# A three-stage transformer stack on one core: when the third and fourth batch's attention starts, and which engine makes the low weight parts

## The chip, the core and the metric

One core of one Trainium2 chip. The time is that of one execution in device microseconds; the kernel before was run three times. One of these runs was also profiled, and every number below that is not one of the three times is of that execution. TensorE is called PE in the rows, VectorE DVE, ScalarE ACT, GpSimd POOL and SyncE SP; SP only issues DMAs here.

## The reference

```python
# 1. attention over 32 memory slots: 4 batches, 8 heads, 576 tokens, head width 64
a = softmax(phi, axis=2)                       # over the tokens' 32 slots
k_m, v_m = a.T @ k, a.T @ v                    # per batch and head: 32 x 64
attn = softmax(q @ k_m.T / 8) @ v_m            # 2304 rows of 512
# 2. a dense layer pair, 512 -> 2048 -> 512, with ELU
h = x @ w_in
x = where(h > 0, h, exp(min(h, 0)) - 1) @ w_out
# 3. eight experts, 512 -> 1024 -> 512, two per token
logits = x @ w_gate + log1p(exp(x @ w_noise)) * noise
# the best two experts of each token, softmax of their logits as weights
out[mask] += weight * (relu(x[mask] @ w1[e]) @ w2[e])
```

## The kernel before

Everything is one loop over 160 iterations. Iterations 0 to 63 are the dense pair: 16 per block of tokens (blocks of 4, 5, 4 and 5 tiles of 128 tokens, one block per batch, `u["blk"]`), and each makes 128 of the 2048 hidden features. Iterations 64 to 159 are the experts. An iteration `i` of the dense pair holds, on PE, `layer1` (L992: 12 matmuls in two halves, each half into one of two PSUM banks called `ph`), and then `layer2` (L1042 to L1044) of iteration `i - 2`: for each tile of the block three matmuls of 512 columns into that tile's accumulator bank `acc`. The products are split: each operand is a high part (`bh`, `gh`, `ah`, `th`) and a low part (`bl`, `gl`, `al`, `tl`), and three of the four cross products are summed. ACT takes two exponentials out of `ph` (L997, L998) and DVE finishes the ELU (L1006, then L1007, which reads `ph`); only when L1007 has read a half is its bank free for the next iteration's `layer1`. The high part of the weight chunk that `layer2` will need two iterations later is made by ACT (L571), the low part by `prep_lo` (L577).

The attention of batch 1, 2 and 3 is no stage of its own. `attention(b)` is a Python generator; `tick` is called at three places of an iteration (before `layer1`, `""`; within it, `"mid"`; and at the end, `"late"`) and lets the generator go one step, if the kind of step that it asked for (`"pe"`, `"light"`, `"next"`, `"late"`, ...) fits the place. A step puts a few instructions into the engines' queues there. Two queues of generators matter: `heads` (the attention, and the last gating) goes first, `tails` (the gating of blocks 0 and 1) after it. A batch's attention pools phi, k and v (L175 transposes, L193), takes scores (L314 into a side bank, L322 to L324 on DVE), normalizes them (L338 to L341), turns them back (L345) and makes high and low parts (`tl`, L350).

The side work on PE needs PSUM banks besides the accumulators. While a block of 5 tiles is in `layer2` there is one only, `px` (`single()`); with 4 tiles there are two, `px` and `acc4`. The folding of the attention's values into the first layer's weights (`fold`, L491, every fourth iteration) uses them too: ACT and DVE take `fh` and `fl` out of the banks (L137, L138).

The gating (`gating(blk, ...)`, L652 to L815) of a finished block runs beside the next block: logits (L642), top two experts, positions by a matmul with a triangle of ones (L768 to L772, one step, one side bank), then on POOL the slots (L786 to L806) and one small indirect DMA per 128 entries (L815), paced by `beat` (L624): at most two per iteration. The engines run their queues in order, so an instruction that waits holds all behind it on its engine.

Of the kernel before, what the change touches and what calls it, by code (L numbers as in the profile page):

```python
# [9 lines left out]
F32 = mybir.dt.float32  # L10
# [5 lines left out]
OP = mybir.AluOpType  # L16
# [4 lines left out]
P = 128  # L21
NB, NH, S, HD, NM = 4, 8, 576, 64, 32
# [4 lines left out]
H = S // 2  # L27
# [15 lines left out]
def moe_stack_kernel(ctx, tc, phi, kv, kvt, q, wmlp, wgn, noise, wmoe, out):  # L43
# [27 lines left out]
    def single():  # L71
        return len(banks["tags"]) == 1
# [42 lines left out]
    def att_loads(b):  # L115
        return ([lambda: load_phi(b)] + [lambda w=w, c=c: load_kv(b, w, c) for w in range(2) for c in range(2)]
                + [lambda h=h: load_q(b, h) for h in range(2)])
# [21 lines left out]

    def attention(b):  # L140
        first = b == 0
        for _ in range(0 if first else 1 if b == 1 else 2):
            yield "gap"
        ph = att["phi", b]
        nmx = sm.tile([P, 2], F32, tag="nmx", name="nmx")
# [110 lines left out]
        sbs = {}  # L256
# [75 lines left out]
        def grow_t(h, g):  # L332
            act.activation(sbs[h, g], sbs[h, g], AF.Exp, scale=0.125)

        def normalize_t(h, g):
            sb = sbs[h, g]
            su = sm.tile([P, 16], F32, tag="ssu", name="ssu", bufs=2)[:, :H // 32]
            dve.tensor_reduce(out=su, in_=sb, axis=AX, op=OP.add)  # L338
            dve.tensor_scalar(su, su, 1e-9, None, op0=OP.add)
            dve.reciprocal(su, su)  # L340
            (dve if b == 3 else pool).tensor_tensor(sb, sb, su[:, :, None].to_broadcast([P, H // 32, NM]), op=OP.mult)  # L341

        def turn_t(h, g):
            back = sbs[h, g, "back"] = ap_.tile([P, 1024], F32, tag="cvm", name="back", bufs=2)[:, :H]
# [2 lines left out]

        def lower_t(h, g):
            hi, lo = (t[:, g, h * H:(h + 1) * H] for t in xt)
            dve.tensor_tensor(lo, sbs[h, g, "back"], hi.bitcast(F32), op=OP.subtract)  # L350

        if first:
            scores(0)
            grow(0)
            scores(1)
            grow(1)
            load_to(3)
            keep([("a", 0), ("a", 1)])
            load_phi(1)
            pooled([1])  # L360
            normalize(0)
            scores(2)
            across([1])
            conv1_hi(pieces(0))
            normalize(1)
            warm(2)
            fold_half(0)
            grow(2)
            normalize(2)
            warm(3)  # L370
            turn(0)
            conv1_lo(pieces(0))
            warm(4)
            turn(1)
            turn(2)
            conv2(pieces(0))
            conv1_hi(pieces(1))
            conv1_lo(pieces(1))
        elif b >= 2:
            yield "gap"  # L380
            for h in range(2):
                if single():
                    if h:
                        grow_t(0, 0)
                    scores_t(h, [0])
                    yield
                    if h:
                        grow_t(0, 1)
                    scores_t(h, [1])
                    yield "next" if h else "pe"  # L390
                else:
                    for g in range(2):
                        scores_t(h, [g])
                        yield "late"
                        grow_t(h, g)
                        if (h, g) != (1, 1):
                            yield "mid"
            if (1, 0) in sbs and single():
                grow_t(1, 0)
                grow_t(1, 1)  # L400
            q0, q1, q2, q3 = [(h, g) for h in range(2) for g in range(2)]
            for steps in ([(normalize_t, q0)], [(normalize_t, q1)], [(turn_t, q0), (turn_t, q1)],
                          [(normalize_t, q2)], [(lower_t, q0), (lower_t, q1)], [(normalize_t, q3)],
                          [(turn_t, q2), (turn_t, q3)], [(lower_t, q2), (lower_t, q3)]):
                yield "light"
                for step, q in steps:
                    step(*q)
        else:
            scores(0)
            yield "late"  # L410
            grow(0)
            yield
            scores(1)
            yield "late"
            grow(1)
            normalize(0)
            yield
            scores(2)
            yield "late"
            grow(2)  # L420
            normalize(1)
            yield
            turn(0)
            yield "late"
            normalize(2)
            yield
            turn(1)
            yield
            turn(2)
# [143 lines left out]
    def prep_lo(parts):  # L573

        for h, c in parts:
            hi, lo = ready[h, c]
            dve.tensor_tensor(lo, raws.pop((h, c)), hi.bitcast(F32), op=OP.subtract)  # L577

# [7 lines left out]
    def tick(slot="", taken=False):  # L588


        place[0] = slot
        kinds = {"": {"pe", "light", "next"}, "mid": {"pe", "mid"}, "late": {"late", "light"}}[slot]
        kinds = kinds - ({"pe", "mid"} if taken else set())
        went = False
        for queue in (heads or tails, tails, sides):
            if queue is sides and slot == "mid" and not taken and not (went and single()):
                kinds = {"mid"}
            while queue:
                gen = queue[0]
                want = wants.get(id(gen)) or {"fetch": "next", "tiles": "late"}.get(gen.__name__, "pe")  # L600
                if want == "gap":
                    if slot != "late":
                        wants[id(gen)] = None
                    break
                if want not in kinds or want == "next" and stepped.get(id(gen)) == i:
                    break
                stepped[id(gen)] = i
                went = True
                try:
                    wants[id(gen)] = next(gen)  # L610
                    if moe.get("pair") or slot == "late":
                        kinds -= {"pe"} & {want}
                    else:
                        kinds -= {want} - {"next"} if slot == "" else kinds
                    break
                except StopIteration:
                    wants.pop(id(queue.pop(0)), None)
# [41 lines left out]
    def gating(blk, rows):  # L659
# [102 lines left out]
        wts = rec.bitcast(F32)  # L762
        if eng is pool:
            pool.tensor_scalar(den, e2, 1.0, 1e-9, op0=OP.add, op1=OP.add)
        yield "next" if blk < 2 else "pe"
        last = blk == len(BLOCKS) - 1
        bk = side_bank()
        pe.matmul(bk[:, :nt * NE + NE].rearrange("p (t e) -> p t e", e=NE), ones,  # L768
# [359 lines left out]
    for i in range(len(flat)):  # L1128
# [3 lines left out]
        if i < len(flat):  # L1132
# [22 lines left out]
                            route(m, flat.index((m, 0)))  # L1155
            if k == late + 4 and f == 2:
                tails.append(overflow_table())
            if k in (1, 2) and f == 0:
                paced = att_loads(k + 1) + paced
            if k < 3 and f == 0:  # L1160
                n = units[k + 1]
                n["need"] = attention(k + 1)
                heads.append(n["need"])
            if k and u["kind"] == "mlp" and f == 0:
                u["x"] = att["x", k]
            j = (i + 2) // 4
# [182 lines left out]
```

## Time and profile before

| what | value |
|---|---|
| three runs: median, lowest, highest | 866.58, 866.22, 867.23 us |
| the profiled execution's time | 866.58 us |
| its span, first to last instruction | 864.8 us |
| PE busy, share of the span | 840.4 us, 97% |
| DVE | 567.5 us, 66% |
| ACT | 438.3 us, 51% |
| POOL | 205.5 us, 24% |
| PE's granted clock over the span | 0.998 of full speed |

The profiled execution is the median run itself; 1.8 us of its time lie outside the span. Busy shares are averages over stages: the dense pair ends at about 400 us and the experts fill the rest. A matmul's busy time ends later than the moment at which the next one can start, so gaps on PE are read from start to start as well.

### The profile page before, as it was taken

Reading aid. Unit: us, or ns where it says so; the run is one execution under the profiler, and the core shown is the slowest. Engines: PE = TensorE matmul, PEld = TensorE weight load, DVE = VectorE, ACT = ScalarE, POOL = GpSimd, SP = SyncE. Lnnn points to the kernel's source line nnn. Section 1 sums busy time; section 2 is a strip of 40 time slices with the busy share of each in tenths; the row PEclk is TensorE's granted clock in tenths of the full one; section 3 lists DMA queues with packets and bytes.
Section 4 is the critical chain, followed back from the end, with each engine's and each line's share of the span. In section 5 each row is a group of like instructions: output and inputs, shape, how many; then the busy total and the mean of one; then the engine's idle time right before and its main releaser. Section 6 shows DMA issues by size and latency. Waiting matters only on the chain. (4 is left out here: it accounts for less than half of the span.)

```text
span 864.8 us, 15414 instructions
## 1 busy us (share of the span) xinstructions
PE 840.4 (97%) x5688; PEld 695.7 (80%) x5691; DVE 567.5 (66%) x1200; ACT 438.3 (51%) x1007; POOL 205.5 (24%) x319
## 2 busy tenths in 40 slices
PE   8999999999999899999999999999999999999995
PEld 5566668777877678888888998898899999899994
DVE  4878888589778897687787664654757354453321
ACT  4867666555655565555656544444534243332311
POOL 0100100002306535031545430341431050110303
PEclk9999999999999999999999999999999999999999
DMA  9996678964852436364898987879995674542404
GB/s 340 362 388 227 223 270 270 325 242 155 298 165 99 98 137 157 99 207 128 245 230 231 283 239 271 226 206 282 257 271 140 197 178 144 160 108 98 60 1 60
DMA packets 100575, 174.65 MB, mean 202 GB/s; under 512 B 14610, under 2 KB 52370, under 8 KB 99474
## 3 DMA queue, kind: packets, MB, share of 16 engines
q1 hardware_dynamic: 90514, 152.93, 55.3%
q0 software_dynamic: 9984, 20.72, 11.7%
q8 instruction: 45, 0.74, 0.4%
q14 instruction: 32, 0.26, 0.1%
HBM read 132.01 MB, written 41.61 MB: 201 GB/s over the span
## 5 line engine op out<-in xcount | busy, mean ns | idle before, releaser
L1042 PE MATMUL acc<-bh,gl 128*128 128x512 f32 (+1 forms) x552 | 219.6, 398 | 0.6 <-DVE rows L1063 0.5
L1043 PE MATMUL acc<-bl,gh 128*128 128x512 f32 (+1 forms) x552 | 216.6, 392 | 0.0
L1044 PE MATMUL acc<-bh,gh 128*128 128x512 f32 (+1 forms) x552 | 216.0, 391 | 0.0
L1021 DVE SCALAR_TENSOR_TENSOR gl<-ph,gh 128x312 fp32r<-128x312 f32 (+2 forms) x128 | 61.5, 481 | 191.8 <-ACT gh L1020 191.8
L571 ACT ACTIVATE bh<-raw 128x512 fp32r<-128x512 f32 x144 | 89.9, 624 | 72.5 <-PE acc L1044 72.4
L1042 PEld LDWEIGHTS acc<-bh,gl 128*128 128x128 f32 (+1 forms) x552 | 102.8, 186 | 26.2 <-issue 6.5
L1044 PEld LDWEIGHTS acc<-bh,gh 128*128 128x128 f32 (+1 forms) x552 | 102.8, 186 | 23.7
L1020 ACT ACTIVATE gh<-ph 128x312 fp32r<-128x312 f32 (+2 forms) x128 | 54.8, 428 | 126.1 <-PE ph L992 125.9
L1043 PEld LDWEIGHTS acc<-bl,gh 128*128 128x128 f32 (+1 forms) x552 | 102.8, 186 | 17.1
L1065 POOL DMA_INDIRECT out<-rows,ids x40 | 64.9, 1622 | 187.8 <-DVE rows L1063 168.0
L577 DVE TENSOR_TENSOR bl<-raw,bh 128x512 fp32r<-128x512 f32 x144 | 99.0, 687 | 5.6 <-ACT bh L571 5.6
L992 PE MATMUL ph<-xl,ah 128*128 128x312 f32 (+2 forms) x512 | 95.2, 308 | 0.0
L992 PE MATMUL ph<-xh,al 128*128 128x312 f32 (+2 forms) x512 | 94.2, 306 | 0.0
L992 PE MATMUL ph<-xh,ah 128*128 128x312 f32 (+2 forms) x512 | 93.5, 305 | 0.0
L992 PEld LDWEIGHTS ph<-xl,ah 128*128 128x128 f32 x512 | 83.5, 189 | 8.9
L992 PEld LDWEIGHTS ph<-xh,al 128*128 128x128 f32 x512 | 79.4, 188 | 0.0
L992 PEld LDWEIGHTS ph<-xh,ah 128*128 128x128 f32 x512 | 78.9, 188 | 0.0
L992 PE MATMUL ph<-tl,fh 128*128 128x288 f32 x256 | 60.5, 317 | 6.3 <-DVE elu L1007 4.7
L577 DVE TENSOR_TENSOR al<-raw,ah 128x512 fp32r<-128x512 f32 x96 | 65.4, 681 | 0.0
L1006 DVE SCALAR_TENSOR_TENSOR elu<-elu 128x288 f32<-128x288 f32 x128 | 58.5, 457 | 9.4 <-ACT elu L998 9.4
L936 POOL DMA_INDIRECT xg<-x2d,ids x35 | 37.3, 1066 | 112.7 <-DMA ids<-lst 70.4
L1013 ACT ACTIVATE gh<-elu 128x576 fp32r<-128x576 f32 (+1 forms) x50 | 33.0, 660 | 58.4 <-DVE elu L1007 58.4
(263 smaller groups left out, 1243.4 us busy)
## 6 DMA issues: line engine op xcount, KB each, us to landing
raw<-in_wmoe SPq DMA_DIRECT2D x48, 1024.0 KB, 6.7
raw<-in_wmlp SPq DMA_DIRECT2D x32, 512.0 KB, 7.2
raw<-wxa SPq DMA_DIRECT2D x12, 1024.0 KB, 6.9
raw<-wxb SPq DMA_DIRECT2D x12, 1024.0 KB, 7.6
xs<-xg SPq DMA_DIRECT2D x35, 256.0 KB, 8.6
xq<-xs SPq DMA_DIRECT2D x140, 64.0 KB, 4.4
kv<-in_kv SPq DMA_DIRECT2D x8, 1024.0 KB, 10.2
out<-zrow SPq DMA_DIRECT2D x13, 512.0 KB, 9.7
```

What stands on the lines that cost most here:

```text
L571: act.activation(ready[h, c][0], raws[h, c], AF.Copy)
L577: dve.tensor_tensor(lo, raws.pop((h, c)), hi.bitcast(F32), op=OP.subtract)
L936: pool.indirect_dma_start(out=xg, out_offset=None, in_=x2d[:rows], in_offset=bass.IndirectOffsetOnAxis(ap=n["ids"][:, t, 0:1], axis=0))
L992: pe.matmul(ph, w, x, start=k == 0, stop=k == len(terms) - 1)
L1006: dve.scalar_tensor_tensor(m, t[:, 0, o], 1.0, m, op0=OP.add, op1=OP.mult)
L1013: act.activation(gh[:, o], m, AF.Copy)
L1020: act.activation(gh[:, o], ph, AF.Relu)
L1021: dve.scalar_tensor_tensor(gl[:, o], ph, 0.0, gh[:, o].bitcast(F32), op0=OP.max, op1=OP.subtract)
L1042: pe.matmul(acc, gl[:, o], wh, start=f == 0, stop=False)
L1043: pe.matmul(acc, gh[:, o], wl, start=False, stop=False)
L1044: pe.matmul(acc, gh[:, o], wh, start=False, stop=f == u["nf"] - 1)
L1065: d = pool.indirect_dma_start(out=out, out_offset=bass.IndirectOffsetOnAxis(ap=ids[:m, t, 0:1], axis=0), in_=r, in_offset=None, compute_op ...
```

## The change

Four things, all in iterations 9 to 63. The attention of batch 2 is handed to `heads` in iteration 13 in place of 16 and that of batch 3 in iteration 26 in place of 32 (its two "gap" steps fall away as well, so its first step comes in iteration 13 and about iteration 25 to 26), and the loads of phi, k, v and q for them are queued in iterations 9 and 23. The scores and exponentials of these two batches are written so that a step fits both one and two side banks. In iterations 16 to 63 the low part of layer 2's weight chunk (L577) is made by GpSimd instead of VectorE, and so are the attention's low parts (L350) of batches 2 and 3 and batch 3's normalization (L341). The gating's position step of blocks 0 and 1 gets a kind of its own, `"bank"`, which is not taken in a `tick` whose iteration has just folded.

```diff
--- before.py
+++ after.py
@@ -139,7 +139,7 @@
 
     def attention(b):
         first = b == 0
-        for _ in range(0 if first else 1 if b == 1 else 2):
+        if b == 1:
             yield "gap"
         ph = att["phi", b]
         nmx = sm.tile([P, 2], F32, tag="nmx", name="nmx")
@@ -338,7 +338,7 @@
             dve.tensor_reduce(out=su, in_=sb, axis=AX, op=OP.add)
             dve.tensor_scalar(su, su, 1e-9, None, op0=OP.add)
             dve.reciprocal(su, su)
-            (dve if b == 3 else pool).tensor_tensor(sb, sb, su[:, :, None].to_broadcast([P, H // 32, NM]), op=OP.mult)
+            pool.tensor_tensor(sb, sb, su[:, :, None].to_broadcast([P, H // 32, NM]), op=OP.mult)
 
         def turn_t(h, g):
             back = sbs[h, g, "back"] = ap_.tile([P, 1024], F32, tag="cvm", name="back", bufs=2)[:, :H]
@@ -347,7 +347,7 @@
 
         def lower_t(h, g):
             hi, lo = (t[:, g, h * H:(h + 1) * H] for t in xt)
-            dve.tensor_tensor(lo, sbs[h, g, "back"], hi.bitcast(F32), op=OP.subtract)
+            pool.tensor_tensor(lo, sbs[h, g, "back"], hi.bitcast(F32), op=OP.subtract)
 
         if first:
             scores(0)
@@ -378,26 +378,26 @@
             conv1_lo(pieces(1))
         elif b >= 2:
             yield "gap"
+            raw_ = []
             for h in range(2):
                 if single():
-                    if h:
-                        grow_t(0, 0)
-                    scores_t(h, [0])
-                    yield
-                    if h:
-                        grow_t(0, 1)
-                    scores_t(h, [1])
-                    yield "next" if h else "pe"
-                else:
                     for g in range(2):
+                        if len(raw_) > 1:
+                            grow_t(*raw_.pop(0))
                         scores_t(h, [g])
-                        yield "late"
-                        grow_t(h, g)
-                        if (h, g) != (1, 1):
-                            yield "mid"
-            if (1, 0) in sbs and single():
-                grow_t(1, 0)
-                grow_t(1, 1)
+                        raw_.append((h, g))
+                        yield "next" if h and g else "pe"
+                    continue
+                for g in range(2):
+                    scores_t(h, [g])
+                    yield "late"
+                    for a in raw_ + [(h, g)]:
+                        grow_t(*a)
+                    raw_.clear()
+                    if (h, g) != (1, 1):
+                        yield "mid"
+            for a in raw_:
+                grow_t(*a)
             q0, q1, q2, q3 = [(h, g) for h in range(2) for g in range(2)]
             for steps in ([(normalize_t, q0)], [(normalize_t, q1)], [(turn_t, q0), (turn_t, q1)],
                           [(normalize_t, q2)], [(lower_t, q0), (lower_t, q1)], [(normalize_t, q3)],
@@ -574,7 +574,7 @@
 
         for h, c in parts:
             hi, lo = ready[h, c]
-            dve.tensor_tensor(lo, raws.pop((h, c)), hi.bitcast(F32), op=OP.subtract)
+            (pool if 15 < c < 64 else dve).tensor_tensor(lo, raws.pop((h, c)), hi.bitcast(F32), op=OP.subtract)
 
 
 
@@ -589,20 +589,20 @@
 
 
         place[0] = slot
-        kinds = {"": {"pe", "light", "next"}, "mid": {"pe", "mid"}, "late": {"late", "light"}}[slot]
-        kinds = kinds - ({"pe", "mid"} if taken else set())
+        kinds = {"": {"pe", "light", "next", "bank"}, "mid": {"pe", "mid"}, "late": {"late", "light"}}[slot]
+        kinds = kinds - ({"pe", "mid", "bank"} if taken else set())
         went = False
         for queue in (heads or tails, tails, sides):
             if queue is sides and slot == "mid" and not taken and not (went and single()):
                 kinds = {"mid"}
             while queue:
                 gen = queue[0]
-                want = wants.get(id(gen)) or {"fetch": "next", "tiles": "late"}.get(gen.__name__, "pe")
+                want = wants.get(id(gen)) or {"fetch": "next", "tiles": "late", "attention": "light" if id(gen) not in wants else "pe"}.get(gen.__name__, "pe")
                 if want == "gap":
                     if slot != "late":
                         wants[id(gen)] = None
                     break
-                if want not in kinds or want == "next" and stepped.get(id(gen)) == i:
+                if want not in kinds or want in ("next", "bank") and stepped.get(id(gen)) == i:
                     break
                 stepped[id(gen)] = i
                 went = True
@@ -762,7 +762,7 @@
         wts = rec.bitcast(F32)
         if eng is pool:
             pool.tensor_scalar(den, e2, 1.0, 1e-9, op0=OP.add, op1=OP.add)
-        yield "next" if blk < 2 else "pe"
+        yield "bank" if blk < 2 else "pe"
         last = blk == len(BLOCKS) - 1
         bk = side_bank()
         pe.matmul(bk[:, :nt * NE + NE].rearrange("p (t e) -> p t e", e=NE), ones,
@@ -1155,12 +1155,14 @@
                             route(m, flat.index((m, 0)))
             if k == late + 4 and f == 2:
                 tails.append(overflow_table())
-            if k in (1, 2) and f == 0:
-                paced = att_loads(k + 1) + paced
-            if k < 3 and f == 0:
-                n = units[k + 1]
-                n["need"] = attention(k + 1)
+            if i in (9, 23):
+                paced = att_loads(2 + i // 16) + paced
+            if i in (0, 13, 26):
+                n = units[1 + i // 13]
+                n["need"] = attention(1 + i // 13)
                 heads.append(n["need"])
+                if i == 0:
+                    wants[id(n["need"])] = None
             if k and u["kind"] == "mlp" and f == 0:
                 u["x"] = att["x", k]
             j = (i + 2) // 4
```

Where the instructions stand. The first place is PE's queue around the fold of iteration 18 (`ph` and `px` are PSUM banks, `raw` a weight chunk, `kmF` the pooled keys of batch 2, `acc` an accumulator). Before:

```order
L491 MATMUL ph<-raw,vT 32x512
L491 MATMUL px<-raw,vT 32x512
L1042 MATMUL acc_1537<-bh,gl 128x512
L1043 MATMUL acc_1537<-bl,gh 128x512
L1044 MATMUL acc_1537<-bh,gh 128x512
L992 MATMUL ph<-tl,fh 128x288 x2
```

and now:

```order
L491 MATMUL ph<-raw,vT 32x512
L491 MATMUL px<-raw,vT 32x512
L1042 MATMUL acc_1617<-bh,gl 128x512
L1043 MATMUL acc_1617<-bl,gh 128x512
L1044 MATMUL acc_1617<-bh,gh 128x512
L314 MATMUL px<-q,kmF 32x288 x4
L992 MATMUL ph<-tl,fh 128x288 x2
```

The scores of batch 2 now ask for `px` one tile after the fold has filled it. In the same way the position step of block 0, which stood behind a fold of iteration 39, stands in iteration 33 right behind scores of batch 3, and in the same bank:

```order
L314 MATMUL px<-q,kmF 32x288 x4
L768 LDWEIGHTS ones
L768 MATMUL px<-run,ones 128x40
L770 LDWEIGHTS tri
L770 MATMUL px<-g_oh,tri 128x32
L992 MATMUL ph<-tl,fh 128x288 x2
```

The second place is DVE's queue from the elementwise work of iteration 42 to that of 43. Before (the queue of PE has a fold in between, whose two L138 stand here):

```order
L1007 SCALAR_TENSOR_TENSOR elu<-ph,elu 128x288
L322 STREAM_TRANSPOSE sbt<-px 128x288
L323 TENSOR_REDUCE smx<-sbt 128x9
L324 TENSOR_TENSOR sbt<-sbt,smx 128x288
L138 TENSOR_TENSOR fl<-acc_3472,fh 128x512
L138 TENSOR_TENSOR fl<-px,fh 128x512
L338 TENSOR_REDUCE ssu<-sbt 128x9
L339 TENSOR_SCALAR ssu<-ssu 128x9
L340 RECIPROCAL ssu<-ssu 128x9
L341 TENSOR_TENSOR sbt<-sbt,ssu 128x288
L1025 TENSOR_TENSOR gl<-elu,gh 128x512
L577 TENSOR_TENSOR bl<-raw,bh 128x512
```

and now:

```order
L1007 SCALAR_TENSOR_TENSOR elu<-ph,elu 128x288
L712 RECIPROCAL g_r<-g_r 128x40
L138 TENSOR_TENSOR fl<-acc_3535,fh 128x512
L138 TENSOR_TENSOR fl<-px,fh 128x512
L1025 TENSOR_TENSOR gl<-elu,gh 128x512
L1006 SCALAR_TENSOR_TENSOR elu<-elu 128x288
```

The attention of batch 3 and the low part have left this stretch. The third place is POOL's queue after the slots of block 0. Before, the slots were followed by the entries alone, with nothing between them:

```order
L806 CAST g_slot_2571<-g_ss1_3206 128x4
L624 COPY tiny_101<-beat_3214 1x1
L815 DMA lst_89<-g_rec_2572,g_slot_2571 19328x2
L624 COPY tiny_101<-beat_3246 1x1
L815 DMA lst_89<-g_rec_2572,g_slot_2571 19328x2
```

and now (from the entry beside iteration 34 on):

```order
L577 TENSOR_TENSOR bl_2864<-raw_2405,bh_2863 128x512
L624 COPY tiny_101<-beat_2898 1x1
L815 DMA lst_89<-g_rec_2255,g_slot_2254 19328x2
L624 COPY tiny_101<-beat_2962 1x1
L815 DMA lst_89<-g_rec_2255,g_slot_2254 19328x2
L577 TENSOR_TENSOR bl_2948<-raw_2405,bh_2947 128x512
L341 TENSOR_TENSOR sbt_2708<-sbt_2708,ssu_2984 128x288
L624 COPY tiny_101<-beat_2989 1x1
L815 DMA lst_89<-g_rec_2255,g_slot_2254 19328x2
L341 TENSOR_TENSOR sbt_2708<-sbt_2708,ssu_3005 128x288
```

The low parts of iterations 34 and 35 and the first two normalizations of batch 3 now stand between the entries of block 0. DVE's transposes of what these two leave (L345) stand right behind the elementwise work of iteration 36, and the pair of the other two normalizations behind that of iteration 38.

## Rows read from the trace of the kernel before

**Rows 1.** The waits of PE: total us, times, longest us.

```profile
PE ph L992 <- DVE elu L1007: 4.7, 4, 1.7
...
PE acc L768 <- DVE fl L138: 1.5, 1, 1.5
...
PE ph L992 <- DVE fl L138: 0.5, 1, 0.5
```

**Rows 2.** Busy us (count) of PE, PEld, DVE, ACT, POOL in 40 us; clock; DMA.

```profile
280.00:320.00 40.00, 35.33 (x214) 27.93 (x213) 35.57 (x90) 22.28 (x65) 17.15 (x43) 1.00 0.39 106
```

**Rows 3.** PE in time: start us, us, line; a logits group, then an undisturbed iteration.

```profile
262.52 0.45 PE L642 MATMUL acc<-wgs,x2T 128*32 128x16 f32 x32
...
316.34 0.51 PE L992 MATMUL ph<-tl,fh 128*128 128x288 f32 x2
...
320.52 0.39 PE L1044 MATMUL acc<-bh,gh 128*128 128x512 f32 x1
320.75 0.42 PE L992 MATMUL ph<-tl,fh 128*128 128x288 f32 x2
```

**Rows 4.** DVE and PE in time, from the fold of iteration 43 to iteration 44.

```profile
284.63 0.68 DVE L138 TENSOR_TENSOR fl<-px,fh 128x512 fp32r<-128x512 f32 x1
...
288.87 0.50 PE L992 MATMUL ph<-tl,fh 128*128 128x288 f32 x2 [1.25 <-DVE elu L1007]
```

**Rows 5.** PE and DVE in time, the fold of iteration 15.

```profile
117.78 0.61 PE L491 MATMUL px<-raw,vT 64*32 64x512 f32 x1
...
120.19 0.68 DVE L138 TENSOR_TENSOR fl<-px,fh 128x512 fp32r<-128x512 f32 x1
```

**Rows 6.** PE in time, the fold of iteration 18 and iteration 19.

```profile
137.00 0.61 PE L491 MATMUL px<-raw,vT 64*32 64x512 f32 x1
...
138.81 0.43 PE L992 MATMUL ph<-tl,fh 128*128 128x288 f32 x2
```

**Rows 7.** PE and DVE in time, scores of batch 2.

```profile
171.80 0.69 PE L314 MATMUL px<-q,kmF 64*32 64x288 f32 x8
...
172.42 0.50 PE L1042 MATMUL acc<-bh,gl 128*128 128x512 f32 x1
172.56 0.48 DVE L322 STREAM_TRANSPOSE sbt<-px 128x288 f32<-128x288 f32 x1 [1.49 <-PE px L314]
```

**Rows 8.** Groups by line: count, busy us, mean ns, idle before.

```profile
L577 DVE TENSOR_TENSOR bl<-raw,bh 128x512 fp32r<-128x512 f32 x144 | 99.0, 687 | 5.6 <-ACT bh L571 5.6
L1006 DVE SCALAR_TENSOR_TENSOR elu<-elu 128x288 f32<-128x288 f32 x128 | 58.5, 457 | 9.4 <-ACT elu L998 9.4
L294 POOL TENSOR_TENSOR sb<-sb,ssu 128x512 f32<-128x512 f32 x4 | 4.2, 1049 | 88.7 <-ACT elu L998 63.3 <-DVE ssu L293 25.4
L341 POOL TENSOR_TENSOR sbt<-sbt,ssu 128x288 f32<-128x288 f32 x4 | 3.6, 911 | 102.4 <-ACT gh L1016 92.1 <-DVE ssu L340 9.6 <-PE ph L992 0.8
```

**Rows 9.** POOL and DVE in time, a normalization of batch 1.

```profile
95.53 1.05 POOL L294 TENSOR_TENSOR sb<-sb,ssu 128x512 f32<-128x512 f32 x1 [5.78 <-DVE ssu L293]
95.81 1.07 DVE L1006 SCALAR_TENSOR_TENSOR elu<-elu 128x288 f32<-128x288 f32 x1
```

**Rows 10.** POOL in time: noisy logits of block 0; its slots; its first entries.

```profile
224.27 0.31 POOL L693 TENSOR_SCALAR g_u<-g_u 128x32 f32<-128x32 f32 x1
...
232.94 0.41 POOL L729 TENSOR_TENSOR g_noisy<-g_noisy,lg 128x32 f32<-128x32 f32 x1
...
266.47 0.21 POOL L786 TENSOR_TENSOR g_rec<-g_rec,g_e 128x4 f32<-128x4 f32 x1 [4.31 <-DVE g_rec L785]
...
270.79 0.18 POOL L624 COPY tiny<-beat 1x1 f32<-1x1 f32 x1
...
275.97 0.17 POOL L624 COPY tiny<-beat 1x1 f32<-1x1 f32 x1
```

**Rows 11.** DVE in time, from a pair of L345 to the end of that iteration's work.

```profile
199.77 0.83 DVE L345 STREAM_TRANSPOSE back<-sbt 128x288 f32<-128x288 f32 x2
...
203.13 0.68 DVE L577 TENSOR_TENSOR bl<-raw,bh 128x512 fp32r<-128x512 f32 x1
```

## The prediction

> **What bounds the kernel now.** I read the page's busy shares first: PE is busy 840.4 of 864.8 us at a granted clock of 0.998 (the table), so the amount of matrix work is the bound, and the change adds and removes none: it moves instructions in PE's queue and takes elementwise work from one engine to another. What it can win is PE's idle time. So the next view is PE's own waits [rows 1]. The largest is `layer1` waiting for L1007: 4.7 us in four waits. It is a wait for a `ph` bank that DVE has not read yet, so DVE is late. Then 1.5 us in which the position step of block 0 (L768) waits for the fold's bank, and 0.5 us in which `layer1` waits for one. The windows show where DVE is late: between 280 and 320 us it is busy 35.57 of 40 us, and there PE has 35.33, the least of all windows but the first and the last [rows 2]. That is iterations 43 to 47, where batch 3's softmax, the gating of block 1 and the low parts meet on DVE. An undisturbed iteration of a four-tile block takes 320.75 - 316.34 = 4.41 us, and a matmul of 0.39 us is followed 0.23 us later by the next, so a wait costs PE some 0.16 us more than its idle row says [rows 3]. The six waits above are worth 6.7 + 6 x 0.16 = 7.7 us.
>
> **What is removed.** In iteration 43 DVE is through with the fold at 284.63 + 0.68 = 285.31; then come a normalization (L338 to L341), L1025, L577 and the elementwise work, and PE, ready at 288.87 - 1.25 = 287.62, waits [rows 4]. The new order leaves only L1025 (0.7) between the fold and L1006: the first half's L1007 would end at about 285.3 + 0.7 + 2 x 0.46 = 286.9, 0.7 us ahead of PE. The later three of these waits hang on the same load, and DVE's queue holds 2.5 to 4.3 us of work per iteration there instead of 4.2 to 6.6 (durations by line, laid on the order). The position step leaves the fold that it waited for, and the wait of 0.5 us goes because batch 2's exponentials no longer stand ahead of the fold's copies on ACT. I take all 7.7 us; if a fold's own delay stays in the 0.5, it is 7.2.
>
> **What is added: first term.** `px` is filled by the fold of iteration 18, and one tile later PE wants it for scores (first place in the order). How long the bank is held: from L491 to the end of L138, 120.87 - 117.78 = 3.09 us [rows 5]. How soon PE comes: 138.81 - 137.00 = 1.81 us [rows 6]. So PE waits about 1.3 us. Not less than 0 (if ACT and DVE were through at once, against every fold of the trace), not more than 2.2, if ACT is behind by one exponential.
>
> **Second term.** In iteration 33 L768 wants `px` right behind scores. L322 frees it at 172.56 + 0.48 = 173.04, where the next matmul came at 172.42 [rows 7]: 0.6, with the signal 0.7 us. From 0.6 if DVE is waiting for it, to 2 if DVE is a copy or two behind.
>
> **What the low parts cost.** 48 subtractions leave DVE, 0.69 us each, 33 us in all. On GpSimd the nearest row is a product of the same 128 x 512 values, 1.05 us, so 50 us; POOL has been busy a quarter of the span [rows 8]. A low part made in iteration i is wanted in iteration i + 2, at least 8.8 us later, which hides 1.05 us. But GpSimd and DVE get into each other's way: while POOL ran such a product, L1006 (two inputs in SBUF) took 1.07 instead of 0.46 us [rows 8, 9]. So each low part can cost DVE between nothing and 0.6 us, against the 0.69 it saves. I take nothing: in an undisturbed iteration L1007 is ahead of PE by 0.7 us or more. That is the cover, and where it is gone it is a rival below.
>
> The Trainium skill speaks against the move: SBUF — State Buffer, "SBUF: two separate sides", says that GpSimd and a VectorE instruction with two SBUF inputs take a shared port pair as an exclusive lock for a whole instruction. Rows 9 agree, 1.07 us; taken as a price for every low part, it is the slower rival. GPSIMD Engine Reference, "4.1 Engine selection", puts two-input elementwise work at about twice VectorE's time. The row is 1.5 times; by that page a low part would be some 1.4 us (an estimate) and the sum about 1 us higher.
>
> **Third term: POOL's queue.** Here a wait takes the place of the old ones. Slots and entries of block 0 now share POOL's queue with low parts and normalizations (third place in the order), and L345 on DVE waits for the normalizations, with L1006 of the next iteration queued behind it. Counted from PE's start of iteration 34: the slots can begin when DVE has copied block 1's last accumulator, about 0.7 (an estimate: the previous iteration's last tile ends at 0). Slots take 270.79 - 266.47 = 4.3 us, an entry (275.97 - 270.79) / 3 = 1.73 us [rows 10]. Up to the second normalization: 0.7 + 4.3 + 4 entries 6.9 + 2 low parts 2.1 + 2 normalizations 1.8 = 15.8. On PE, iteration 34 with a fold is 4.4 + 1.1 (1.81 less one tile of 3 x 0.23, rows 3 and 6) and 35 is 4.4, so iteration 36 begins at 9.9, and POOL is through 5.9 us into it. DVE came to L345 at about 4. From a pair of L345 to the last item of its iteration took 203.13 - 199.77 = 3.4 us [rows 11]; with one short item less and the first half's L1006 and L1007 more it is 3.8. So L1007 is done at 9.7, and PE wants the bank at 4.4 + 4.9 (logits add 0.5, rows 3) = 9.3: 0.4 us lost. The second pair: 4 entries 6.9, 2 low parts 2.1, 2 normalizations 1.8, and two L350, as large as a normalization, 1.8: 12.6 more, 28.4. Iteration 38 begins at 9.9 + 9.3 + 0.4 = 19.6; POOL is through 8.8 into it, L1007 of iteration 39 4.2 later (a fold's two L138 in place of a sum) at 13.0, and PE wants it at 6.0 + 4.9 = 10.9: 2.1 lost. Together 2.5 us. It is 0 if POOL is 2 us quicker (normalizations at 0.67 and entries at 1.5 nearly do it), and 4.5 if each tensor operation there meets the lock.
>
> The rest costs nothing. The noisy logits take 233.35 - 224.27 = 9.1 us on POOL [rows 10], and block 1's stand ahead of the low part of iteration 43. Begun some 4 us into iteration 42, they and it are done at about 14.5, and PE comes for it at 6 + 2 x 4.4 + 1.6 = 16.4. Loads of batches 2 and 3 are issued seven and nine iterations earlier, into buffers whose last readers are long through; they lead their first reader by two or more iterations. The other L350 were 0.46 us each on DVE and have a block's time to spare.
>
> **The sum.** The profiled execution took 866.58 us, which is the median of the three runs: 866.6 - 7.7 + 1.3 + 0.7 + 2.5 = **863.4 us**.
>
> **Rivals.**
> The new waits are hidden. If POOL runs the entries closer together and DVE is waiting for the fold's copies, the third term is 0 and the first two 1: 866.6 - 7.7 + 1 = 859.9. For it: each margin in the third term is under 2 us. Against: POOL has eight entries, four low parts, four normalizations and two L350 in 18 us.
>
> POOL gives it all back. All the bounds are met (2.2 + 2 + 4.5) and the noisy logits of block 1, which share the lock with DVE, run 2 us longer than their margin: 866.6 - 7.7 + 8.7 = 867.6 at worst, with half of it 865.5. For it: POOL's normalizations beside DVE took 0.91 us on the mean. Against: DVE has less to do there than before.
>
> Slower: the lock makes DVE late everywhere. In some 13 iterations (18, 21, 22, 30 to 33, 35 to 38, 58, 59) the new order's DVE work with 0.6 us more reaches the length of PE's iteration. If every low part hits an L1006 there, PE loses 13 x 0.6 = 7.8 us: 871.2. It decides from 8 such iterations on, 863.4 + 4.9 = 868.3. Against: POOL can start a low part only when its high part is there, and DVE is often at work on one-input instructions then.
>
> The change does nothing here: the waits of iterations 43 to 47 come back through other DVE work, 866.6. Its queue there is short, so this is unlikely.
>
> **How the numbers follow.** 0.43 for the forecast (861 to 864.8), 0.25 for hidden waits, 0.17 for POOL giving it back or nothing changing, 0.12 for slower, 0.03 for anything faster still. About 0.2% (1.7 us) is what a measurement of this kernel can tell from no change, so faster means under 864.9 and slower over 868.3: faster 0.71, same 0.17, slower 0.12. The range leaves out most of the slower case and the far end of hidden waits: 859.5 to 867. The forecast's own range is 861 to 864.8.
>
> **What would show it.** In the waits of the changed kernel, L992 on L1007 falls from 4.7 us to 3 or less, and what is left lies at iterations 38 and 40, not 43 to 47. A new wait of L314 on `fl` of about 1.3 us, and L768 on `sbt` of under 1. DVE idle ahead of L345, released by POOL, 1 to 5 us in two places. L1006 shows some durations near 1 us. I am wrong if PE waits for `bl`, if a DMA holds L193 or L150, or if L1007 stalls are spread over many iterations.

## The result and the profile after

The changed kernel is slower. Four runs each, on one chip: 877.6 us (874.66 to 877.99) against 866.9 (866.22 to 868.21) before, ratio 1.0115, 95% interval 1.0101 to 1.0128. The forecast was 863.4, with a range up to 867.0.

From the start of iteration 2 to that of iteration 64 (PE's first L992 of each) before took 398.40 - 32.93 = 365.5 us, the changed kernel 409.11 - 32.25 = 376.9. The experts behind it take the same (457.0 us to PE's last instruction in both), so all of the 11.4 us are in the dense pair. First the page's busy row and its row of the granted clock, then PE's waits (total us, times, longest):

```profile
PE 847.9 (97%) x5691; PEld 699.4 (80%) x5691; DVE 570.6 (65%) x1140; ACT 436.1 (50%) x1007; POOL 277.0 (32%) x379
PEclk9999998999999999999999999999999999999998
```

```profile
PE px L642 <- DVE fl L138: 1.7, 1, 1.7
...
PE px L314 <- DVE fl L138: 1.5, 1, 1.5
PE ph L491 <- DVE elu L1007: 1.5, 3, 1.1
PE acc L314 <- DVE rows L1052: 1.4, 1, 1.4
...
PE ph L992 <- DVE elu L1007: 1.0, 2, 0.7
PE ph L992 <- DVE fl L138: 1.0, 2, 0.7
```

Against [rows 1]: the 4.7 us of L992 on L1007 are down to 1.0 and L768 no longer waits for the fold, as forecast. L314 waits for the fold, 1.5 (forecast 1.3). The folds of five-tile blocks (L491) now wait 1.5 us for L1007. And DVE's busy time is 570.6 us after 567.5, although 60 instructions have left it. The groups by line (count, busy us, mean ns, idle before) show why; compare [rows 8]:

```profile
L1006 DVE SCALAR_TENSOR_TENSOR elu<-elu 128x288 f32<-128x288 f32 x128 | 73.9, 578 | 17.2 <-ACT elu L998 16.9
...
L1007 DVE SCALAR_TENSOR_TENSOR elu<-ph,elu 128x288 f32<-128x288 f32 x100 | 45.8, 458 | 3.4
L1025 DVE TENSOR_TENSOR gl<-elu,gh 128x576 fp32r<-128x576 f32 x32 | 30.5, 952 | 5.7 <-ACT gh L1013 5.0
...
L577 POOL TENSOR_TENSOR bl<-raw,bh 128x512 fp32r<-128x512 f32 x48 | 63.4, 1326 | 103.0 <-ACT bh L571 97.8 <-DMA xq<-xs 4.5 <-POOL g_den L764 0.3
```

L1007 and L1025 in the kernel before:

```profile
L1007 DVE SCALAR_TENSOR_TENSOR elu<-ph,elu 128x288 f32<-128x288 f32 x100 | 45.7, 457 | 3.4
L1025 DVE TENSOR_TENSOR gl<-elu,gh 128x576 fp32r<-128x576 f32 x32 | 23.9, 748 | 6.4 <-ACT gh L1013 5.7
```

L1006 and L1025 (both inputs in SBUF) went from 457 to 578 and from 748 to 952 ns; L1007, of the same size as L1006 but with one input in PSUM, stayed at 458. Over iterations 16 to 63 DVE's instructions exceed the shortest tenth of their kind by 41 us in sum (5 before), 18 of it in L1025 and 16 in L1006, which eats the 33 us that the low parts took off DVE and the 5 of L341 and L350. One case in time, POOL, DVE and PE in iteration 22 (start us, us):

```profile
169.82 1.28 POOL L577 TENSOR_TENSOR bl<-raw,bh 128x512 fp32r<-128x512 f32 x1
...
169.86 1.55 DVE L1006 SCALAR_TENSOR_TENSOR elu<-elu 128x288 f32<-128x288 f32 x1
171.45 0.46 DVE L1007 SCALAR_TENSOR_TENSOR elu<-ph,elu 128x288 f32<-128x288 f32 x1
...
171.96 0.61 PE L491 MATMUL ph<-raw,vT 64*32 64x512 f32 x1 [1.06 <-DVE elu L1007]
```

L1006 starts 0.04 us after a low part and lasts until that is through and 0.3 longer: 1.1 us late, and PE waits 1.06 for the bank that L1007 frees. Last the clock, in windows of 40 us (busy us and counts, then the granted clock), and PE in time:

```profile
120.00:160.00 40.00, 37.79 (x271) 26.95 (x272) 25.93 (x56) 20.04 (x52) 6.43 (x5) 0.91 0.86 275
...
240.00:280.00 40.00, 36.39 (x295) 28.43 (x294) 33.63 (x68) 21.36 (x64) 28.54 (x43) 0.96 0.50 146
```

```profile
145.24 0.69 PE L314 MATMUL px<-q,kmF 64*32 64x288 f32 x8 [1.54 <-DVE fl L138]
...
146.49 0.43 PE L992 MATMUL ph<-th,fh 128*128 128x288 f32 x2
...
147.04 0.68 PE L992 MATMUL ph<-th,fl 128*128 128x288 f32 x2
```

Behind the wait of L314 in iteration 18 matmuls of the same size go from 0.43 to 0.68 us: the clock is at its lower level (1.2 GHz). It is so twice, the second time behind the wait of 1.4 us of L314 on L1052 in iteration 33. Iterations 19 and 34 take 9.74 and 7.11 us; with the same matmuls at the upper level (2.4 GHz) they take 6.63 and 5.54 (in the run of the order alone, below). So 4.7 of the 11.4 us of this execution are the lower clock.

### The profile page after: what moved, and what is told of

Same layout as the page of the kernel before. It is cut to its first block, busy times and chain, and to the rows that moved or that the text cites. A ratio compares the mean times of both kernels' runs of the same rounds, so it can differ in the third digit from the quotient of the medians.

```text
span 875.9 us, 15477 instructions
## 1 busy us (share of the span) xinstructions
PE 847.9 (97%) x5691; PEld 699.4 (80%) x5691; DVE 570.6 (65%) x1140; ACT 436.1 (50%) x1007; POOL 277.0 (32%) x379
## 5 line engine op out<-in xcount | busy, mean ns | idle before, releaser
L577 POOL TENSOR_TENSOR bl<-raw,bh 128x512 fp32r<-128x512 f32 x48 | 63.4, 1326 | 103.0 <-ACT bh L571 97.8
L992 PE MATMUL ph<-xl,ah 128*128 128x312 f32 (+2 forms) x512 | 95.2, 308 | 0.0
L992 PE MATMUL ph<-xh,al 128*128 128x312 f32 (+2 forms) x512 | 94.2, 306 | 0.0
L992 PE MATMUL ph<-xh,ah 128*128 128x312 f32 (+2 forms) x512 | 93.4, 304 | 0.0
L992 PEld LDWEIGHTS ph<-xl,ah 128*128 128x128 f32 x512 | 83.5, 189 | 8.9
L1006 DVE SCALAR_TENSOR_TENSOR elu<-elu 128x288 f32<-128x288 f32 x128 | 73.9, 578 | 17.2 <-ACT elu L998 16.9
L992 PEld LDWEIGHTS ph<-xh,al 128*128 128x128 f32 x512 | 79.4, 188 | 0.0
L992 PEld LDWEIGHTS ph<-xh,ah 128*128 128x128 f32 x512 | 78.9, 188 | 0.0
L577 DVE TENSOR_TENSOR bl<-raw,bh 128x512 fp32r<-128x512 f32 x96 | 65.9, 686 | 0.0
L577 DVE TENSOR_TENSOR al<-raw,ah 128x512 fp32r<-128x512 f32 x96 | 65.4, 682 | 0.0
```

Of the source, the lines that this page charges most:

```text
L577: (pool if 15 < c < 64 else dve).tensor_tensor(lo, raws.pop((h, c)), hi.bitcast(F32), op=OP.subtract)
L992: pe.matmul(ph, w, x, start=k == 0, stop=k == len(terms) - 1)
L1006: dve.scalar_tensor_tensor(m, t[:, 0, o], 1.0, m, op0=OP.add, op1=OP.mult)
```

## The experiments

Theories. **Lock:** POOL's low parts block DVE's two-input instructions, and DVE frees PE's banks late. **Early attention:** the new order asks for banks before they can be free, whatever POOL does. The ratio is to runs of the kernel before on the same chip; "16 to 63" counts iterations 2 to 63 of the profiled execution (before: 365.5 us); L1006 is its mean, longest and the number over 0.6 us.

| run | us | kernel before there, us | ratio (95%) | 2 to 63, us | L1006 ns, longest, over 600 |
|---|---|---|---|---|---|
| kernel before | 866.9 | | | 365.5 | 457, 1070, 1 |
| changed kernel | 877.6 | 866.9 | 1.0115 (1.0101 to 1.0128) | 376.9 | 578, 2195, 20 |
| e1_low_dve | 869.15 | 867.5 | 1.0019 (1.0004 to 1.0034) | 367.2 | 480, 1393, 5 |
| e2_order_alone | 868.89 | 867.5 | 1.0016 (1.0002 to 1.0030) | 366.3 | 455, 1070, 1 |
| e3_pool_alone | 879.04 | 867.5 | 1.0129 (1.0104 to 1.0153) | 378.7 | 572, 2226, 18 |
| e5_held_back | 879.14 | 867.5 | 1.0140 (1.0108 to 1.0173) | 376.8 | 572, 2206, 20 |
| e7_held_all_dve | 867.21 | 866.5 | 1.0012 (1.0000 to 1.0023) | 366.1 | 454, 1071, 1 |
| e8_split | 869.74 | 866.5 | 1.0039 (1.0024 to 1.0054) | 368.3 | 515, 1072, 14 |
| e9_fourth_old | 868.17 | 866.5 | 1.0019 (1.0008 to 1.0029) | 366.1 | 456, 1072, 1 |
| e10_third_old | 870.69 | 866.5 | 1.0042 (1.0025 to 1.0059) | 369.7 | 456, 1071, 1 |
| e11_dve_delay | 872.14 | 866.2 | 1.0067 (1.0051 to 1.0083) | 369.7 | 457, 1069, 1 |
| e12_low_behind | 871.66 | 870.4 | 1.0017 (1.0006 to 1.0027) | 367.2 | 457, 1069, 1 |
| e13_held_low_behind | 873.29 | 870.4 | 1.0037 (1.0022 to 1.0053) | 368.9 | 456, 1072, 1 |
| e14_held_split | 874.96 | 870.4 | 1.0055 (1.0038 to 1.0071) | 371.0 | 521, 1068, 16 |

The kernel before did not take the same everywhere, so the runs are compared by their ratios and not by their times. The one L1006 over 600 ns of the kernel before is that of [rows 9].

### The parts of the change, one at a time

e1 puts the low parts back; e2 also L350 and batch 3's L341, which leaves the order alone; e3 is the kernel before with POOL's low parts alone.

```diff
 e1, e2 (in the changed kernel)
-            (pool if 15 < c < 64 else dve).tensor_tensor(lo, raws.pop((h, c)), ...)
+            dve.tensor_tensor(lo, raws.pop((h, c)), ...)
 e3 (in the kernel before)
-            dve.tensor_tensor(lo, raws.pop((h, c)), ...)
+            (pool if 15 < c < 64 else dve).tensor_tensor(lo, raws.pop((h, c)), ...)
```

> The changed kernel with one line put back: all 48 low parts of layer 2's weights (L577) on DVE again; the early attention and POOL's normalizations stay. Theory 'lock': POOL's low parts make DVE's two-input work slow (L1006 578 instead of 457 ns), and so DVE late for the banks. Then L1006 falls back to about 460 ns, PE's waits on L1007 (2.5 us in all) shrink to under 1, the waits behind the fold get shorter, the clock does not fall, and the time is 862 to 867. Rival 'early attention': the scores come too soon behind the fold and the row copies, whatever DVE has to do; the waits of 1.5 us (L314 on fl) and 1.4 us (L314 on rows) stay, the granted clock falls again, and the time is 872 to 876.

> The changed kernel with every operation back on the engine it had before (L577, L350, and L341 of batch 3 on DVE): the early attention alone. Lock: 861 to 866, as POOL's extra work is gone altogether. Early attention: 872 to 876, with waits of L314 on fl and on rows of over 1 us each. Whatever it gives, this run less the kernel before is the price of the order, and the changed kernel less this run is the price of the engines.

> The kernel before with one line changed: the low parts of iterations 16 to 63 (L577) on POOL, the attention where it was. Lock: L1006 at 570 to 600 ns, new waits of PE on L1007 spread over iterations 18 to 38, time 870 to 875. Early attention: the low parts cost nothing by themselves and take 33 us off DVE, so the waits of iterations 43 to 47 shrink: 861 to 866.

Measured: the low parts cost 1.15% - 0.19% = 0.96%, 8.3 us, in the new order, and 1.29%, 11.2 us, in the old one; L350 and L341 on POOL cost 0.3 us (e1 against e2, within their intervals); the order costs 0.16%, 1.4 us. These prices include what the clock lost: between iterations 2 and 64 it did not fall in the profiled executions of e1 and e2, and it fell twice in that of e3. So the lock theory holds for the size of the loss (e3 even came out above its 870 to 875), but e1 and e2 missed their 862 to 867 and 861 to 866: the order gains nothing. In e3, DVE, POOL and PE in iteration 43:

```profile
294.98 1.96 DVE L1006 SCALAR_TENSOR_TENSOR elu<-elu 128x288 f32<-128x288 f32 x1
295.34 1.27 POOL L577 TENSOR_TENSOR bl<-raw,bh 128x512 fp32r<-128x512 f32 x1
...
297.57 0.82 PE L992 MATMUL ph<-tl,fh 128*128 128x288 f32 x2 [3.23 <-DVE elu L1007]
```

The wait that the change was to remove there ([rows 4], 1.25 us) is 3.23 with POOL's low parts in the old order. This L1006 even began 0.4 us ahead of the low part, while POOL issued an entry (L815, until 295.31), and still lasted until the low part was through. In the kernel before none of the 13 L1006 beside an entry alone took over 0.48 us. How it comes to be held is open. Why the order alone gains nothing, the windows of e2 show:

```profile
240.00:280.00 40.00, 36.17 (x334) 28.22 (x335) 35.71 (x85) 23.06 (x69) 16.32 (x30) 1.00 0.65 172
280.00:320.00 40.00, 40.00 (x278) 33.28 (x277) 30.81 (x71) 24.69 (x70) 13.31 (x40) 1.00 0.32 106
```

Between 280 and 320 us PE now has no idle time (35.33 busy before, [rows 2]). But DVE's full stretch has moved to 240 to 280, 35.71 us, and PE stands there for 3.8. Its waits in e2 from start to start (such a gap less the matmul's usual distance): 1.36 and 1.61 at the two L314, 0.89 at L768, 1.4 in iterations 22 to 27 and 3.4 in 36 to 39, 8.7 in all, where 7.7 were removed.

### Half as long instructions on POOL

```diff
 e8 (in the changed kernel, shortened; r is the raw chunk)
-            pool.tensor_tensor(lo, r, hi, op=OP.subtract)
+            for o in (slice(0, 256), slice(256, 512)):
+                pool.tensor_tensor(lo[:, o], r[:, o], hi[:, o], op=OP.subtract)
```

> The changed kernel, but each of POOL's 48 low parts is two instructions of 256 columns instead of one of 512. If a DVE instruction with two SBUF inputs has to wait for the end of the POOL instruction that runs (a lock for a whole instruction), it now waits for half as long: L1006's mean falls from 578 to some 500 to 540 ns, the worst one from 1.5 to about 1.0 us, and the time from 877.6 to 871 to 875. If the two engines merely share what SBUF gives, or if POOL's queue is what is late, L1006 stays near 578 ns and the time at 876 to 879.

```profile
L1006 DVE SCALAR_TENSOR_TENSOR elu<-elu 128x288 f32<-128x288 f32 x128 | 66.0, 515 | 19.9 <-ACT elu L998 19.9
...
L577 POOL TENSOR_TENSOR bl<-raw,bh 128x256 fp32r<-128x256 f32 x96 | 77.7, 831 | 94.4 <-ACT bh L571 82.9 <-PE ph L992 10.8 <-POOL g_den L764 0.3
```

POOL is busy longer for it (77.7 against 63.4 us), and by the ratios the kernel is some 0.76%, 6.6 us, quicker, more than was expected. The longest L1006 beside a half takes 1.02 us, not 2.2 (the 1.07 of the table is that of [rows 9] again). If POOL's queue had been late, or the two engines had shared a bandwidth, POOL's longer busy time should have made this run no faster. The Trainium skill says so of the cause (SBUF — State Buffer, "SBUF: two separate sides"): a VectorE instruction with two SBUF inputs and one of GpSimd that reads SBUF exclude each other for a whole instruction. The trace agrees (L1006 1.55 us beside a low part of 1.28; L1007 with its PSUM input 0.46). The L1006 of e3 that began ahead of its low part and was held all the same is not explained by this.

### Steps held back

```diff
 e5 (changed kernel), e7 (order alone), e14 (changed kernel with the split)
-        kinds = kinds - ({"pe", "mid", "bank"} if taken else set())
+        kinds = kinds - ({"pe", "mid", "bank"} if taken else {"pe", "bank"} if slot == ""
+            and (i == 34 or i > 15 and i % 4 == 3 and single()) else set())
```

> The changed kernel, but no scores or position step is begun in the place right behind a fold of a five-tile block, nor right behind the end of a block (iteration 34): such a step goes one place later. POOL's low parts stay. The two waits of L314 (1.73 and 1.61 us from start to start) should go, up to new ones of a few tenths. If the fall of the granted clock (6.83 us from 146.97 on, 3.41 us from 245.96 on, together worth some 4.9 us) follows from those waits, it goes too: 877.6 - 3.3 - 4.9 = 869.4. If it follows from the scores themselves or from the fold, the clock still falls in the same iterations: 877.6 - 3.3 = 874.3. Lock: the other waits (L1007, L642 on fl) stay as they are, so not under 868.

> The early attention with every operation on the engine that it had before, and no scores or position step in the place right behind a fold of a five-tile block or behind the end of a block. Against the order alone (868.9) the two waits of L314 (1.36 and 1.61 us) and most of that of L768 (0.89) should go: 865 to 867 if nothing takes their place. If the first late scores push the softmax into the fold and the logits of iterations 36 to 40, as POOL's did in the run with POOL's low parts, 868 to 870.

> The changed kernel with both edits that worked against a part of its loss: POOL's low parts as two instructions of 256 columns, and no scores or position step right behind a fold of a five-tile block or the end of a block. If the wait for a whole POOL instruction was what made the run with held-back steps slow (879), this one gets the gain that the holding back gave with everything on DVE (1.7 us): 869.7 - 1.7 = 868. If POOL's queue is what is late there (L345 waited 3.4 us for L341 in that run), the wait of 4 us in iteration 39 stays and the time is 872 to 876.

In e5 the wait of L314 for the fold goes (that for L1052 shrinks to 0.3), and with them the fall of the clock in iterations 19 and 34. The time fell neither to 869 nor to 874: a fold's L491 waits 2.3 us for L1007 in iteration 26, the softmax comes one iteration later, and now the prediction's third term appears, in iteration 39 of e5:

```profile
273.41 0.99 POOL L815 DMA_INDIRECT lst<-g_rec,g_slot  x1 [0.16 <-issue]
274.43 1.30 POOL L577 TENSOR_TENSOR bl<-raw,bh 128x512 fp32r<-128x512 f32 x1
275.67 0.68 POOL L341 TENSOR_TENSOR sbt<-sbt,ssu 128x288 f32<-128x288 f32 x1
276.38 0.48 DVE L345 STREAM_TRANSPOSE back<-sbt 128x288 f32<-128x288 f32 x1 [3.43 <-POOL sbt L341]
...
279.58 0.82 PE L992 MATMUL ph<-tl,fh 128*128 128x288 f32 x2 [3.98 <-DVE elu L1007]
```

DVE waits 3.4 us for a normalization that stands behind an entry and a low part on POOL, and PE 4.0 for the L1007 behind it; the clock falls there. e14 has the same wait (3.62, PE 4.63). In the changed kernel L345 waited 0.2. With everything on DVE (e7) the two waits of L314 go or shrink (to 0.7), but others take their place (1.3 us of L491 on L1007 in iteration 26, 1.0 twice at L642 in 37 and 38). The times of e7 and e2 lie 1.7 us apart, but they were taken where the kernel before took 866.5 and 867.5 us. By the ratios holding back gives 0.04%, 0.3 us, well within the intervals, and iterations 2 to 63 say 0.2 us: no gain is shown. The 1.7 us that e14 was expected to win from it, and did not, were this difference. e7 is as close to the kernel before as any version came. None beats it.

### One batch early at a time

e9 and e10 have every operation where it was, and `i in (0, 13, 32)` or `(0, 16, 26)` for `i in (0, 13, 26)`.

> Everything on the engine it had before; only the third batch's attention is early (iteration 13), the fourth's begins in iteration 32 as before. The third's early start costs a wait of 1.36 us at L314 in iteration 18 and 0.5 to 1 in 22 and 23, and saves the 0.5 in iteration 19; the waits of iterations 38 and 43 to 47 stay: 867.5 to 869. If the early third batch is harmless, 866 to 867.

> Everything on the engine it had before; only the fourth batch's attention is early (iteration 26), the third's begins in iteration 16. The waits of iterations 43 to 47 go (5.9 us from start to start, with 1.6 at 38), those of the order alone in 32, 33 and 36 to 39 come (0.9 + 1.6 + 1.0 + 0.5 + 0.6 + 1.3 = 5.9): 866 to 868. If the third batch's early start made DVE late in 36 to 39 only through the slots of block 0, and these waits are shorter here, 863 to 866.

e9 came out as expected; L1007's waits are 3.1 us in it, and new ones of 1.2 (L314) and 0.9 (L175 on L1052) take their place. e10 missed: it is the slowest order, as batch 2's L175 now stands right behind folds (2.9 us in two waits). Neither half of the order carries a hidden gain.

### The place of the low part on DVE

```diff
 e12 (kernel before); e13: "i in (25, 26) or 34 < i < 41", in e7
-            ahead = nxt[:1] if 61 < i < 64 else nxt
+            ahead = nxt[:1] if 61 < i < 64 else [] if 41 < i < 48 else nxt
```

> The kernel before with one thing changed: in iterations 42 to 47 DVE makes the low part of layer 2's weights behind the elementwise work (L1006, L1007) and not ahead of it; it still has a whole iteration to spare. If the place of the low part in DVE's queue is what matters to PE (the release of the ph bank stands behind it), the waits of iterations 43 to 47 fall from 5.9 us to 3 to 4.5, and the time is 864 to 866. If DVE has simply too much to do there, only the first of these waits gets shorter, by 0.7: 866 to 866.5. Slower only if a low part comes too late for PE, which the iteration in between rules out.

> The early attention with everything on the engine it had before and with the steps held back (867.2), and in iterations 25, 26 and 35 to 40 the low part behind L1006 and L1007 on DVE. By the place in the queue the waits of 26 (1.4 us) and of 36 to 40 (4.1 us) shrink by 2 to 3 us in all: 864 to 866, which would be the fastest of all. By sheer load on DVE, which has no idle time from 252 to 277 us in that run, 0.7 us less: 866.5.

Both missed: they are slower than what they start from (e13 starts from e7). In e12, DVE and PE in iteration 44:

```profile
292.08 0.69 DVE L1025 TENSOR_TENSOR gl<-elu,gh 128x512 fp32r<-128x512 f32 x1
...
293.79 0.52 DVE L1006 SCALAR_TENSOR_TENSOR elu<-elu 128x288 f32<-128x288 f32 x1 [1.02 <-ACT elu L998]
...
294.86 0.53 PE L992 MATMUL ph<-tl,fh 128*128 128x288 f32 x2 [1.76 <-DVE elu L1007]
```

DVE now stands idle for 1.02 us ahead of L1006, until ACT's L998 is through. In the kernel before the low part (0.69) stands in that gap. So moving a low part away there buys idle time, not an earlier L1007. It is not so everywhere: in iteration 43 of e12 the first L1006 stands right behind L1025, without idle time, and comes 0.6 us sooner after the fold.

### Does a wait bring the clock down?

```diff
 e11 (kernel before, shortened; scr is a tile that nothing else reads)
+        [later(lambda: dve.tensor_tensor(scr, scr, scr, op=OP.add))
+         for _ in range({(1, 1): 2, (1, 2): 3, (1, 3): 4, (2, 0): 6}.get((b, j), 0))]
         for g in gs: later(lambda g=g: halve(...))
```

> The kernel before with additions that compute nothing needed, on DVE right ahead of the copies of four folds: 2, 3, 4 and 6 of them (some 0.7 us each) in iterations 18, 22, 26 and 30. PE then has to wait for the fold's bank in or after these iterations, some 2, 2, 3 and 4.5 us, with POOL's low parts on DVE and the attention where it was. If the granted clock falls because PE stood still, it falls behind the longer of these waits, 3 us and more, and perhaps behind those of 2; each fall costs 1.5 to 3.5 us beyond the wait. If the falls come from the early scores or from POOL's work, the clock stays at 1.0 through all four and the time is that of before plus the waits alone, 867.5 + 8 to 11.

```profile
200.00:240.00 40.00, 36.60 (x276) 29.82 (x276) 35.09 (x78) 22.67 (x60) 10.32 (x26) 1.00 0.59 199
```

```profile
217.66 0.53 PE L992 MATMUL ph<-tl,fh 128*128 128x288 f32 x2 [2.94 <-DVE fl L138]
```

Inconclusive: the first two delays cost PE nothing new, and behind a wait of 2.94 us the clock stayed at 1.00. Waits of 2.2 and 2.3 us were followed by a fall in e3 and e8, the 1.4 us of L314 on L1052 in the changed kernel too, but not in e1 and e2. What besides the wait decides is open. The clock also falls where the change has no part: ahead of iteration 2 in the profiled executions of e2, e3, e5, e13 and e14 (from 17.8 to 28.0 us on), and in the experts in e13 (444.5 us). And 19 executions of the kernel before alone, those beside e1 to e5, had granted clocks from 0.992 (869.35 us) to 0.997 (866.03 us). So it is not shown that the 4.7 us of clock in the changed kernel's profile come from the change.

## Why the prediction was wrong

**"What the low parts cost: I take nothing"** is the step that failed: they cost 8.3 us in the new order, what the clock lost with them included. The lock was seen in [rows 9] and priced at up to 0.6 us for each low part. In e3, where only the low parts are on POOL, DVE's excess over the shortest tenth (reckoned as above) is 38 us; less the 5 before, over 48, that is 0.70 for each, and up to 1.1 us for the single one shown above. The operations of the attention (L341, L350) have their part too: in e1 the excess is 11 us. Two things made it more than the row said. A low part took 1.33 us, not the 1.05 of the product taken as nearest. The Trainium skill's factor of about two (GPSIMD Engine Reference, "4.1 Engine selection"), set aside in the prediction, was nearly right: 1326 against 687 ns, 1.9 times. And an L1006 that begins beside an entry can be held through the low part behind it, 2.2 us at worst; L1025 (by as much in sum as L1006) and L339 are held as well. The cover (L1007 0.7 us ahead of PE) is less than one such delay. The slower rival named this mechanism, with a chance of 0.12 and 7.8 us. Of the 10.5 us that the profiled execution of the changed kernel loses against e2's in iterations 2 to 63, some 5.5 are longer waits of PE (gaps of 14.2 us against 8.7 from start to start) and 4.7 the clock, which the rival lacked.

**The saving of 0.69 us a low part** that stood against the lock was not worth all of that either: in places the low part on DVE lies in the gap ahead of L1006 (e12), and L1006's idle time behind ACT went from 9.4 us to 16.9.

**Removed, 7.7 us:** right in its place: in e2 all four waits of L992 on L1007 in iterations 43 to 47 are gone, in the changed kernel the last of them is left, 0.7 us in place of 1.7. **First and second term:** 1.36 and 0.89 us in e2 against 1.3 and 0.7. **What was missing** is 1.61 at the L314 that takes `acc4` while DVE copies rows out of it (L1052), and 4.8 us in iterations 22 to 27 and 36 to 39: the attention's DVE work was counted where it left, not where it arrived. That makes the order 1.4 us slower, where the prediction's 7.7 removed, less its first and second term, make it 5.7 faster.

**Third term, 2.5 us:** did not occur as described in the changed kernel (L345 waits 0.2 us for POOL). The mechanism is real; it came with 3.4 and 3.6 us as soon as the softmax was one iteration later (e5, e14).

**The lower clock**, 4.7 us in the profiled execution, was in no step and no rival, and whether the change causes it is open. It is not the same in all: the run of 874.66 us had a granted clock of 0.995 over its span, the other three 0.991.

## What to carry to other kernels

Before work is moved to GpSimd, look which VectorE instructions with two SBUF inputs run at the same time and whether a release that PE waits for stands behind them; price one such meeting at the whole GpSimd instruction, and keep these short. Work that fills the gap in which an engine waits for another can be free where it is, as in iteration 44 here. When a step is moved earlier, add its instructions to the queue where they arrive, and every bank that it asks for there, before the waits that it leaves behind are counted as won.

## What the runs showed of the hardware that was not expected

A VectorE instruction with one SBUF input of 9 columns (L339, 173 ns on the mean before) took 436 to 1756 ns in the changed kernel in the four of its eight instances that ran beside a low part, a normalization or an L350 of GpSimd, and 173 to 176 in the other four. So this small one-input instruction is held too. One of the four:

```profile
263.84 1.30 POOL L577 TENSOR_TENSOR bl<-raw,bh 128x512 fp32r<-128x512 f32 x1
264.19 1.00 DVE L339 TENSOR_SCALAR ssu<-ssu 128x9 f32<-128x9 f32 x1
```

The clock went to its lower level behind PE waits of 1.4 to 1.5 us in one execution, and did not behind one of 2.94 in another.
